# Infini-attention plus gated layer on one Trainium2 core: the second block's key features are turned by VectorE and moved within SBUF, and the key and query columns are put in another order

## The chip, the cores and the metric

The kernel runs on one core of a Trainium2 chip. The core has five engines that run their own instruction streams and wait for one another through semaphores: TensorE (PE in the profile; its weight loads are shown apart as PEld), VectorE (DVE), ScalarE (ACT), GpSimd (POOL) and SyncE (SP). SP issues most of the transfers here, POOL issues some; the transfers run on 16 DMA engines. SBUF is the working memory of 128 partitions, PSUM the memory of eight banks into which TensorE writes, DRAM the large memory outside.

The metric is the device time of one execution in microseconds (us), lower is better. Three executions of the kernel before took 670.75, 671.38 and 671.44 us; the median is 671.38 us.

## What is computed

```python
x = A_x                                   # 1 x 2048 x 448
xn = _layernorm(x, axis=-1)
return x + A_ref(xn, wq, wk, wv, wo, beta) + B_ref(xn, w_gate, w_up, w_down)

# A_ref: 16 heads of 28; the 2048 tokens are 4 blocks of 512
phi = lambda t: jnp.where(t > 0, t + 1.0, jnp.exp(t))
for s in range(4):
    qs, ks, vs = q[:, :, s], k[:, :, s], v[:, :, s]
    p = softmax(qs @ ks.T * scale + mask)             # inside the block
    a_dot = p @ vs
    a_mem = (phi(qs) @ M) / (phi(qs) @ z + 1e-6)      # what earlier blocks left
    outs.append(g * a_mem + (1 - g) * a_dot)
    M = M + einsum("bhld,bhle->bhde", phi(ks), vs)    # 28 x 28 for each head
    z = z + phi(ks).sum(tokens)
# B_ref: down(sigmoid(xn @ w_gate) * (xn @ w_up)), 1792 wide
```

The part that the change touches is the memory `M`, `z`: for each of the blocks 0, 1 and 2 the key features `phi(ks)` are multiplied with the values, summed over the block's 512 tokens. That sum runs over the partitions of a matmul, so the tokens have to lie on the partitions, whereas the keys come out of their projection with the columns (heads and their 28 rows) on the partitions and the tokens along the row. The key features have to be turned by 90 degrees first.

## The kernel before

**Stages.** A front stage goes through the four blocks `b` of 512 tokens. In each block it makes the values (`values`, four groups of 128 tokens, 11 matmuls each) and then the keys and queries (`keys_queries`, called for `c` = 0 to 6: seven chunks of 128 of the 896 key and query columns, keys first, 11 matmuls each with 512 moving columns). The precision is that of float32, made from a high and a low part of each operand, so each weight is split into a high part by ACT and a low part by POOL (`split_qk`). Behind the front stage lies a long stage in which the gated layer's matmuls, the attention inside the blocks and the output projection are interleaved by a table of ticks. The change edits nothing in the tick table.

**What sets the order.** PE, ACT and DVE execute the front stage in the order in which the code is written. SP and POOL are ordered by the framework's scheduler, and both issue transfers strictly one after another. Block 0 is written out by hand ahead of the loop up to its third group of values.

**The keys of a block.** For a key chunk `c` (0 to 3; the fourth has 64 key columns), `keys_queries` leaves the key features in a tile `e` (columns by tokens, 128 x 512): ACT copies the high part to `qk` (L413) and makes the exponential (L417, L418), DVE the low part (L419) and the feature (L424). At `k` = 3 and `k` = 5 `key_rows` has PE transpose two chunks each (L434, 16 transposes of 128x128 a block), and ACT copies them from PSUM to `kn` (L436). After the seventh chunk `update(b)` multiplies: 64 small matmuls (L445) with 28 columns of `kn` as weights and 32 columns of the values `vst` moving, and DVE adds the four strips to the memory `mst` (L452, L454).

**What else the prediction speaks of.** In block 0 the tokens of block 1 are normalised ahead: `statistics(1)` and `statistics(2)` (L324 to L326) are ready-made ahead of the first chunk, `normalise(1, k - 1)` (L350) makes the rows `xn`, of which POOL copies a tail (L356), and `turn(1, k - 3)` has PE transpose them (L103). For blocks 2 and 3 DVE turns the rows in 32x32 squares into a staging space (L359), and `spread` moves the squares with 16 transfers of 32 partitions each, 8 from SP and 8 from POOL (L374). From block 2 on `load_features` (L460, four transfers from SP) fetches the query features of the block before, which `keys_queries` wrote to DRAM (`fd`, L427), and `recall` (L467) multiplies them with the memory, right behind the block's first chunk.

## Time and profile before

| what | value |
|---|---|
| three executions | 670.75, 671.38, 671.44 us |
| the profiled execution, its own time | 671.5 us |
| its span, first to last instruction | 669.6 us |
| PE busy | 663.7 us (99% of the span) |
| DVE busy | 571.4 us (85%) |
| ACT, POOL busy | 336.1 us (50%), 147.4 us (22%) |
| transposes of the key features L434, x48 | 6.4 us of busy time |
| memory updates L445, x384 | 3.9 us |
| memory reads L467, x96 | 4.9 us |
| granted TensorE clock, whole span | 1.000 |

The share of busy time is no measure of a margin by itself: matmuls overlap, and a matmul that starts late because of a wait can still be drawn as one piece with those around it. In the prediction the rows of the timeline are read by their starts: the time from the start of one piece of PE work to the start of the next is what that piece cost. A row of the timeline gives the start in us from the span's start, the duration in us, the engine, the line of the kernel before, the operation, output and inputs, shapes, and how many instructions are merged into the row; an idle time ahead of it, with what ended it, stands in brackets.

### The profile page before, as it was taken

How to read it: one execution, taken by the hardware profiler on the slowest of the kernel's cores; microseconds unless marked ns; L12 is line 12 of the kernel's file. 1: busy time of each engine (PE TensorE's matmuls, PEld its weight loads, DVE VectorE, ACT ScalarE, POOL GpSimd, SP SyncE). 2: the span in 40 equal slices, each digit the busy share in tenths (PEclk: the TensorE clock that was granted, in tenths of full speed). 3: DMA queues.
4: the chain of work that ended last, by engine and by line, in shares of the span. 5: the costliest groups of instructions: out<-in, count | busy, mean ns of one | idle time of the engine just before them, and what ended most of it. 6: DMA issues, size and time to landing. Idle time of an engine off the chain costs nothing.

```text
span 669.6 us, 11201 instructions
## 1 busy us (share of the span) xinstructions
PE 663.7 (99%) x3922; PEld 553.2 (83%) x3922; DVE 571.4 (85%) x987; ACT 336.1 (50%) x560; POOL 147.4 (22%) x354
## 2 busy tenths in 40 slices
PE   8999999999999999999999999999999999999997
PEld 7888888778888888788787878788887887888897
DVE  6986695878999899899998999899998997999864
ACT  4848474423556455455645546455544644545220
POOL 3502210002222222233122322222122122321000
PEclk9999999999999999999999999999999999999999
DMA  8537788995523432324243423426243352323442
GB/s 321 221 128 251 238 287 284 309 273 197 144 73 88 109 93 73 103 57 105 74 96 103 89 72 57 128 52 141 57 103 64 92 115 57 86 78 80 112 153 97
DMA packets 48767, 88.09 MB, mean 132 GB/s; under 512 B 6856, under 2 KB 22856, under 8 KB 48200
## 3 DMA queue, kind: packets, MB, share of 16 engines
q1 hardware_dynamic: 45048, 79.01, 39.1%
q0 software_dynamic: 3520, 8.26, 6.1%
q8 instruction: 31, 0.51, 0.3%
q14 instruction: 24, 0.20, 0.1%
q10 hardware_dynamic: 144, 0.11, 0.0%
HBM read 52.89 MB, written 32.64 MB: 128 GB/s over the span
## 4 chain that ended last, share of the span: by engine, by line
PE 97%; DVE 2%; DMA 0%; ACT 0%; issue 0%; DVEq 0%
PE pgu L260 42%; PE pd L184 21%; PE pp L412 11%; PE st L704 6%; PE pa L790 5%; PE po L889 5%; PE pv L392 5%; PE pk L434 1%; PE pmm L445 1%; PE n L467 1%; DMA acc<-in_x 0%; DVE stats L324 0%; PE pt L103 0%; DVE xn L350 0%; DVE xs L110 0%
## 5 line engine op out<-in xcount | busy, mean ns | idle before, releaser
L260 PE MATMUL pgu<-xs,wgu 128*128 128x512 f32 x1232 | 301.2, 392 | 0.0
L260 PEld LDWEIGHTS pgu<-xs,wgu 128*128 128x128 f32 x1232 | 228.7, 188 | 46.6 <-issue 2.5
L184 PE MATMUL pd<-wdn,hh 128*128 128x448 f32 x672 | 155.3, 366 | 0.0
L184 PEld LDWEIGHTS pd<-wdn,hh 128*128 128x128 f32 x672 | 122.7, 188 | 11.6 <-issue 0.8
L719 POOL TENSOR_SCALAR_AFFINE_SELECT w<-w 128x256 f32<-128x256 f32 (+1 forms) x160 | 76.1, 479 | 224.0 <-ACT w L708 157.6
L772 ACT ACTIVATE w<-w 128x1024 f32<-128x1024 f32 (+1 forms) x96 | 87.8, 915 | 58.3 <-DVE w L768 58.1
L708 ACT ACTIVATE w<-st 128x512 f32<-128x512 f32 x128 | 75.6, 592 | 60.1 <-PE st L704 59.8
L768 DVE TENSOR_TENSOR w<-w,mb 128x1024 f32<-128x1024 f32 (+1 forms) x96 | 100.6, 1054 | 0.8
L726 DVE TRANSPOSE_TENSOR_REDUCE mx<-w 128x32 f32<-128x1024 f32 x64 | 78.9, 1233 | 4.9 <-POOL w L719 4.9
L412 PE MATMUL pp<-xs,wqk 128*128 128x512 f32 x308 | 73.7, 393 | 0.2 <-DVE kn L473 0.2
L186 DVE TENSOR_TENSOR acc<-pd,acc 128x448 f32<-128x448 f32 x112 | 67.4, 602 | 4.0 <-PE pd L184 4.0
L283 ACT ACTIVATE hh<-sg 128x512 fp32r<-128x512 f32 x56 | 35.3, 631 | 67.7 <-DVE sg L277 44.6
L412 PEld LDWEIGHTS pp<-xs,wqk 128*128 128x128 f32 x308 | 57.2, 188 | 12.9 <-issue 0.8
L704 PE MATMUL st<-qk 84*128 84x128 f32 (+3 forms) x256 | 62.0, 313 | 0.0
L267 ACT ACTIVATE sg<-pgu 128x512 f32<-128x512 f32 x56 | 33.2, 592 | 45.0 <-PE pgu L260 44.9
L704 PEld LDWEIGHTS st<-qk 84*128 84x128 f32 x256 | 47.9, 189 | 8.7 <-issue 1.4
L277 DVE SCALAR_TENSOR_TENSOR sg<-sg,pgu 128x512 f32<-128x512 f32 x56 | 37.7, 673 | 10.1 <-PE pgu L260 9.9
L754 DVE STREAM_TRANSPOSE mb<-top 128x1024 f32<-128x1024 f32 x32 | 39.5, 1234 | 3.3 <-POOL top L751 3.2
L286 DVE SCALAR_TENSOR_TENSOR hh<-sg,hh 128x512 fp32r<-128x512 f32 x56 | 38.2, 681 | 0.2 <-ACT hh L283 0.2
L419 DVE TENSOR_TENSOR qk<-pp,qk 128x512 fp32r<-128x512 f32 x28 | 19.2, 686 | 22.2 <-ACT e L417 21.6
L790 PE MATMUL pa<-w,vv 128*32 128x128 f32 (+3 forms) x512 | 37.8, 436 | 0.0
L392 PE MATMUL pv<-wv,xs 128*128 128x448 f32 x176 | 37.4, 367 | 0.3 <-POOL wv L508 0.2
(113 smaller groups left out, 607.2 us busy)
## 6 DMA issues: line engine op xcount, KB each, us to landing
qk<-qd SPq DMA_DIRECT2D x192, 112.0 KB
qd<-qk SPq DMA_DIRECT2D x28, 512.0 KB
raw<-in_w_ffn SPq DMA_DIRECT2D x14, 512.0 KB
acc<-in_x SPq DMA_DIRECT2D x5, 896.0 KB
vd<-vst SPq DMA_DIRECT2D x4, 1024.0 KB
vv<-vd SPq DMA_DIRECT2D x16, 256.0 KB
od<-w POOLq DMA_DIRECT2D x16, 256.0 KB, 4.1
sums<-od SPq DMA_DIRECT2D x32, 128.0 KB
```

Of the source, the lines that this page charges most:

```text
L184: T.matmul(pd[:, :D], l, r, start=n == 0, stop=n == len(mms) - 1)
L186: V.tensor_add(acc[b][:, t, :], pd[:, :D], acc[b][:, t, :])
L260: T.matmul(dst, wgu[f][:, w, side * P:(side + 1) * P], xs[b][:, a, :], start=n == 0, stop=n == len(TERMS) - 1)
L392: T.matmul(pv[:, :D], xs[b][:, a, t * P:(t + 1) * P], wv[w], start=n == 0, stop=n == len(TERMS) - 1)
L412: T.matmul(pp, wqk[c][:, w, :], xs[b][:, a, :], start=n == 0, stop=n == len(TERMS) - 1)
L704: T.matmul(st[:, at:at + L - kb * P], self.qk[:KS, 1, h, kb * P:(kb + 1) * P], self.qk[:KS, 0, h, kb * P:], start=True, stop=True)
L708: A.activation(w, st, AF.Copy)
L719: G.affine_select(d, d, pattern=pattern, base=0, channel_multiplier=-1, compare_op=ALU.is_ge, fill=MASK)
L726: V.tensor_reduce(self.mx[:, 32 * h:32 * h + 32], w3[:, h, :2 * L].rearrange("p (b n) -> p b n", n=32), axis=mybir.AxisListType.X, op=ALU. ...
L768: V.tensor_sub(w, w, m)
L772: A.activation(w, w, AF.Exp, scale=SCALE)
L790: T.matmul(pa[32 * j:32 * j + 32, kb * P:], self.vv[:, kb, 32 * j:32 * j + 32], self.pairs[j // 2].block(j % 2, kb), start=kb == 0, stop=k ...
```

## The change

**Columns.** The 448 key columns and the 448 query columns are now projected in the order row-major over heads (all 16 heads' row 0, then all heads' row 1, and so on) instead of head by head. The order is made when the weights are split: `split_qk` reads the raw weights with a step of 28 elements. One chunk of 128 columns now draws on the whole 448 raw columns of its side, so the raw weights lie in two tiles of 448 columns (keys, queries) and are loaded by eight transfers in pieces of 512 bytes (one of 64 columns a side), instead of seven chunks in pieces of 2 KB. The query side uses the space of `phi`. The chunks' splits come one chunk later (`split_qk(c + 3)` behind chunk `c`), and `statistics(2)` stands behind block 0's second chunk instead of ahead of its first. The readers of keys and queries in DRAM follow: a load of query features is now one run of 8 KB a partition (L503), and the last block's four loads are issued together.

**The memory update.** In all three blocks the values are now the weights (32 columns) and the key features move (28 columns, one head's rows, 16 elements apart). The result is the transposed memory, so DVE adds it in one instruction to a new tile `memory` and turns that in squares into `mst` (one more instruction), in place of four strips.

**Block 1.** `EXCHANGED = (1,)`: the 16 PE transposes of block 1 and the four ACT copies behind them are gone. DVE turns the four chunks `e` in 32x32 squares (L450) into the staging space that `spread(2)` has just emptied (the fourth into a tile of `e`), and 24 transfers within SBUF (12 from SP, 12 from POOL, 32 partitions each) bring the squares to their places in `kn`: 16 behind chunk 2, 8 behind chunk 3. `update(1)` is called behind the matmuls of the next block's first values instead of behind block 1's last chunk.

On PE, in blocks 1 and 2 (`pp` are the key and query chunks, `pk` the transposes, `pmm` the update, `pv` the values), before:

```order
L412 MATMUL pp<-xs_66,wqk_117 128x512 x11
L434 MATMUL pk<-ident,e 128x128 x8
L412 MATMUL pp<-xs_66,wqk_118 128x512 x11
...
L412 MATMUL pp<-xs_66,wqk_120 128x512 x11
L445 MATMUL pmm<-vst,kn 28x32 x64
L392 MATMUL pv<-wv,xs_67 128x448 x44
```

and now:

```order
L417 MATMUL pp<-xs_66,wqk_117 128x512 x11
L417 MATMUL pp<-xs_66,wqk_118 128x512 x11
...
L417 MATMUL pp<-xs_66,wqk_120 128x512 x11
L395 MATMUL pv<-wv,xs_67 128x448 x11
L490 MATMUL pmm<-kn,vst 32x28 x64
L395 MATMUL pv<-wv,xs_67 128x448 x33
```

The transposes are gone, and the update stands one group of values later.

On SP, from block 1's keys to block 2 (`qd` and `fd` are the stores of keys, queries and query features, `vd` that of the values, `stage<-acc_71` is `spread(3)`), before:

```order
L420 DMA qd_80<-qk 128x1024 x4
L427 DMA fd_84<-e 64x512
...
L460 DMA phi<-fd_84 28x4x512 x3
L398 DMA vd_89<-vst 128x2048
L374 DMA stage<-acc_71 32x4x128
```

and now:

```order
L425 DMA qd_80<-qk 128x1024 x3
L462 DMA kn<-phi 32x3x128 x8
L425 DMA qd_80<-qk 128x1024
L432 DMA fd_84<-e 64x512
L464 DMA kn<-e 32x128 x4
...
L377 DMA stage<-acc_71 32x4x128
L503 DMA phi<-fd_84 28x2048 x4
L401 DMA vd_89<-vst 128x2048
```

Twelve transfers of key features stand between the stores of chunks 2 and 4, and the four loads of query features now stand behind the first transfer of `spread(3)`.

On DVE, in block 0 (`acc_70` and `acc_71` are the tokens of blocks 1 and 2), before:

```order
L326 TENSOR_SCALAR vh_328<-mv_327 128x4
L324 BN_STATS stats_341<-acc_71 128x6
L325 BN_AGGR mv_342<-stats_341 128x2
...
L326 TENSOR_SCALAR vh_343<-mv_342 128x4
L419 TENSOR_TENSOR qk<-pp,qk 128x512
L424 SCALAR_TENSOR_TENSOR e<-pp,e 128x512
...
L625 TENSOR_SCALAR gate_n<-gate 128x4
...
L350 TENSOR_SCALAR xn<-acc_70,mv_327,y_338 128x16x7x4
```

and now:

```order
L329 TENSOR_SCALAR vh_328<-mv_327 128x4
L424 TENSOR_TENSOR qk<-pp,qk 128x512
L429 SCALAR_TENSOR_TENSOR e<-pp,e 128x512
...
L674 MEMSET memory 128x128
...
L678 TENSOR_SCALAR gate_n<-gate 128x4
...
L327 BN_STATS stats_397<-acc_71 128x6
L328 BN_AGGR mv_398<-stats_397 128x2
...
L329 TENSOR_SCALAR vh_399<-mv_398 128x4
L353 TENSOR_SCALAR xn<-acc_70,mv_327,y_338 128x16x7x4
```

The nine instructions of `statistics(2)` have moved from ahead of the first chunk's work to just ahead of the first rows `xn` of block 1.

The diff, cut to what this speaks of:

```diff
+EXCHANGED = (1,)
...
+        memory = sb.tile([P, HG, 32], F32, name="memory", bufs=1)
+        kn_blocks = kn.rearrange("p t n -> p (t n)")[:, :NT * D].rearrange("p (m t r) -> p m t r", t=NT, r=32)
...
         def values(b, t):
             pv = bank("pv", "p")
             value_terms(b, t, pv, EARLY[1] if b == 0 else TERMS)
+            if t == 0 and b - 1 in EXCHANGED:
+                update(b - 1)
             store_values(b, t, pv)
...
+        def turn_keys(e, et):
+            rows = et.shape[0]
+            V.transpose(et.rearrange("p (q t r) -> p t q r", q=4, t=NT),
+                        e[:rows].rearrange("p (t q n) -> p t q n", q=4, t=NT))
+
+        def send_keys(b, et=None):
+
+            to = kn_blocks.rearrange("p m t r -> p m (t r)")
+            src = stages[b + 1][:, :3 * L].rearrange("p (c q n) -> p c q n", c=3, q=4)
+            for q in range(4):
+                for i in range(4 if et is None else 2):
+                    queue = nc.sync if i % 2 else nc.gpsimd
+                    strip = slice(32 * i, 32 * i + 32)
+                    if et is None:
+                        queue.dma_start(to[32 * q:32 * q + 32, i:12:4, :], src[strip, :, q, :])
+                    else:
+                        queue.dma_start(to[32 * q:32 * q + 32, 12 + i, :], et[strip, P * q:P * (q + 1)])
...
         def update(b):
...
-                        T.matmul(pmm[32 * i:32 * i + DH, 32 * j:32 * j + 32], kn[:, t, DH * h:DH * (h + 1)],
-                                 vst[:, t, h, :], start=t == 0, stop=t == NT - 1)
...
+                        T.matmul(pmm[32 * i:32 * i + 32, 32 * j:32 * j + DH], vst[:, t, h, :], rows[t][h],
+                                 start=t == 0, stop=t == NT - 1)
+            p3, m3 = pmm[:, :P].rearrange("p (j c) -> p j c", c=32)[:, :, :DH], memory[:, :, :DH]
+            if b == 0:
+                V.tensor_copy(m3, p3)
+            else:
+                V.tensor_add(m3, p3, m3)
+            V.transpose(mst[(b + 1) % 2].rearrange("p j c -> p (j c)"), memory.rearrange("p j c -> p (j c)"))
...
+        raw_qk = [space.rearrange("p t n -> p (t n)")[:, :4 * D].rearrange("p (w n) -> p w n", w=4)
+                  for space in (stage, features())]
+        for side in range(2):
+            for c in range(4):
+                to, at = (P * c, 0) if side == 0 else (max(P * c - 64, 0), 64 if c == 0 else 0)
+                n = min(P, D - to) if side == 0 else P - at
+                nc.sync.dma_start(raw_qk[side][:, :, to:to + n],
+                                  w_qk[c + 3 * side].rearrange("p (w n) -> p w n", w=4)[:, :, at:at + n])
+            if side == 0:
+                nc.sync.dma_start(acc[1], x_block(1))
...
         def split_qk(c):
...
+                r = raw_qk[side].rearrange("p w (h r) -> p w r h", h=H)[:, :, r0:r1, :]
...
+                A.activation(hi, r, AF.Copy)
+                G.tensor_sub(lo, r, hi.bitcast(F32))
...
             for t in range(3 if b == 0 else 0, NT):
                 values(b, t)
                 if b == 0:
-                    split_qk(t)
                     mv, vh = statistics(1, 0, NT)
...
-                    st[2] = statistics(2, 0, NT)
...
-                if b == 0 and c + 4 < 7:
-                    split_qk(c + 4)
+                if b == 0 and c + 3 < 7:
+                    split_qk(c + 3)
+                if b == 0 and k == 1:
+                    st[2] = statistics(2, 0, NT)
...
-                    for i in range(NG):
-                        if k == (2, 3, 4, 4)[i]:
-                            load_features(b, i, phi)
+                    for i in range(NG if k == 4 else 0):
+                        load_features(b, i, phi)
...
-                if k in (3, 5):
+                if b in EXCHANGED:
+                    exchange(b, c)
+                elif k in (3, 5):
                     for c in (k - 3, k - 2):
                         key_rows(c, e[c])
-                if k == 6:
+                if k == 6 and b not in EXCHANGED:
                     update(b)
```

`exchange(b, c)` turns chunk 0 at `c` = 1, chunks 1 and 2 at `c` = 2 with the first 16 transfers, and chunk 3 at `c` = 3 with the other 8.

More of the change, by code (lines that the diff above doesn't have):

```diff
@@ L436, in key_rows, with turned, exchange @@
             A.activation(kn[:, :, c * P:c * P + n], pk.rearrange("p (t n) -> p t n", t=NT)[:, :, :n], AF.Copy)
+        def turned(b, c):
+            space = stages[b + 1].rearrange("p (c n) -> p c n", n=256)
+            return space[:, 2 * c:2 * c + 2, :].rearrange("p c n -> p (c n)")
+        def turn_keys(e, et):
[13 more added lines that the diff above has]
+                        queue.dma_start(to[32 * q:32 * q + 32, 12 + i, :], et[strip, P * q:P * (q + 1)])
+        def exchange(b, c):
+            if c == 1:
+                turn_keys(e[0], turned(b, 0))
+            elif c == 2:
+                turn_keys(e[1], turned(b, 1))
+                turn_keys(e[2], turned(b, 2))
+                send_keys(b)
+            elif c == 3:
+                et = sb.tile([P, L], F32, name="e", bufs=4)
+                turn_keys(e[3], et[:64])
+                send_keys(b, et)
         def update(b):
             pmm = bank("pmm", "m")
+            if b in EXCHANGED:
+                rows = [[kn_blocks.rearrange("p m t (c h) -> p m t c h", h=H)[:, :, t, :, h] for h in range(H)]
+                        for t in range(NT)]
+            else:
+                rows = [[kn[:, t, h:D:H] for h in range(H)] for t in range(NT)]
             for j in range(HG):
@@ L510, in split_qk @@
         def split_qk(c):
-            r = raw_qk[c].rearrange("p (c n) -> p c n", c=4)
-            A.activation(wqk[c][:, 0:4, :], r, AF.Copy)
-            G.tensor_sub(wqk[c][:, 4:8, :], r, wqk[c][:, 0:4, :].bitcast(F32))
+            for side in range(2):
+                j0, j1 = max(P * c, D * side), min(P * (c + 1), D * (side + 1))
+                if j0 >= j1:
+                    continue
+                r0, r1 = ((j - D * side) // H for j in (j0, j1))
+                r = raw_qk[side].rearrange("p w (h r) -> p w r h", h=H)[:, :, r0:r1, :]
+                hi, lo = (wqk[c][:, w:w + 4, j0 - P * c:j1 - P * c].rearrange("p w (r h) -> p w r h", h=H)
+                          for w in (0, 4))
+                A.activation(hi, r, AF.Copy)
+                G.tensor_sub(lo, r, hi.bitcast(F32))
         warm = bank("warm", "gu")
@@ L621 @@
                     if b == 0:
+                        V.memset(memory, 0.0)
                         A.activation(gate, gate, AF.Exp, scale=-1.0)
@@ L633 @@
                         phi = features()
-                    for i in range(NG):
-                        if k == (2, 3, 4, 4)[i]:
-                            load_features(b, i, phi)
+                    for i in range(NG if k == 4 else 0):
+                        load_features(b, i, phi)
                     if k > 4:
@@ L684, in load @@
                 for n in range(2):
[L685 to L687 removed]
+                    rows = qd[self.s][D * (1 - n):D * (2 - n), parts[n], :].rearrange("(r h) f -> r h f", h=H)
+                    nc.sync.dma_start(self.qk[DH * c:DH * (c + 1), n].bitcast(F32), rows[:, self.h0:self.h0 + 2, :])
         def block(self, h, kb):
```

24 lines of the change are left out of this document (4 added, 20 removed).

## The prediction

> **What bounds the kernel now.** I read the page first, then the chain of waits, then the timeline of each engine over the first 140 us.
>
> ```profile
> span 669.6 us, 11201 instructions
> PE 663.7 (99%) x3922; PEld 553.2 (83%) x3922; DVE 571.4 (85%) x987; ACT 336.1 (50%) x560; POOL 147.4 (22%) x354
> PE 97%; DVE 2%; DMA 0%; ACT 0%; issue 0%; DVEq 0%
> ```
>
> TensorE (PE) sets the end: 97% of the chain. Work taken off PE is won in full, and a wait put in front of PE in the front stage is lost in full, since no idle time lies behind it to take it up. The profiled execution took 671.5 us, the span and 1.9 us around it; the median of the runs is 671.4, so 0.1 is taken off at the end.
>
> The timeline of PE over blocks 0, 1 and the start of 2, where all edits lie:
>
> ```profile
> 19.68 10.14 PE L412 MATMUL pp<-xs,wqk 128*128 128x512 f32 x44
> 29.66 1.21 PE L434 MATMUL pk<-ident,e 128*128 128x128 f32 x8
> 30.71 0.64 PE L103 MATMUL pt<-ident,xn 128*128 128x128 f32 x4
> 31.10 2.77 PE L412 MATMUL pp<-xs,wqk 128*128 128x512 f32 x11
> ...
> 51.11 10.16 PE L412 MATMUL pp<-xs,wqk 128*128 128x512 f32 x44
> 61.11 1.03 PE L434 MATMUL pk<-ident,e 128*128 128x128 f32 x8
> 61.90 5.26 PE L412 MATMUL pp<-xs,wqk 128*128 128x512 f32 x22
> 67.01 1.03 PE L434 MATMUL pk<-ident,e 128*128 128x128 f32 x8
> 67.80 2.77 PE L412 MATMUL pp<-xs,wqk 128*128 128x512 f32 x11
> 70.49 1.29 PE L445 MATMUL pmm<-vst,kn 128*28 128x32 f32 x128
> 71.71 9.14 PE L392 MATMUL pv<-wv,xs 128*128 128x448 f32 x44
> 80.69 2.68 PE L412 MATMUL pp<-xs,wqk 128*128 128x512 f32 x11
> 83.30 1.22 PE L467 MATMUL n<-phi,mst 28*32 28x512 f32 x32
> ```
>
> From start to start: four chunks cost 10.00 us (51.11 to 61.11), so 2.50 each; the update 1.22 (70.49 to 71.71); a group of values 8.98 / 4 = 2.245; block 2's first chunk with its wait 2.61.
>
> **Term 1, the transposes that go: -1.88 us.** Block 1's keys take 19.38 us now (51.11 to 70.49). Without the transposes they are seven chunks, 7 x 2.50 = 17.50. The four PSUM banks of the chunks allow this: DVE's last use of a chunk ends some 2.7 us behind its last matmul (the row of 60.60 below, against 58.61 = 51.11 + 3 x 2.50), far less than the 7.5 us until chunk 6 starts in the same bank. The four ACT copies that go were off the path.
>
> **Term 2, the statistics of block 2, moved: +2.96 us.** This looks like bookkeeping, and I think it is the largest term. The rows that carry it, from the timelines of DVE, ACT and POOL in block 0:
>
> ```profile
> 21.26 0.17 DVE L326 TENSOR_SCALAR vh<-mv 128x4 f32<-128x4 f32 x1
> 21.34 0.62 DVE L324 BATCH_NORM_STATS2 stats<-acc 128x6 f32<-128x448 f32 x1
> 24.59 0.69 DVE L419 TENSOR_TENSOR qk<-pp,qk 128x512 fp32r<-128x512 f32 x1
> 26.00 0.72 DVE L343 TENSOR_TENSOR tm<-y 128x4 f32<-128x4 f32 x1
> 28.01 0.96 DVE L625 TENSOR_SCALAR gate_n<-gate 128x4 f32<-128x4 f32 x1
> 30.08 0.50 DVE L350 TENSOR_SCALAR xn<-acc,mv,y 128x448 f32<-128x448 f32 x1
> ...
> 21.67 1.28 ACT L586 ACT_TABLE_LOAD   x1
> 23.55 0.59 ACT L417 ACTIVATE e<-pp 128x512 f32<-128x512 f32 x1
> ...
> 25.41 1.30 POOL L513 TENSOR_TENSOR wqk<-wqk_raw,wqk 128x512 fp32r<-128x512 f32 x1 [2.79 <-ACT wqk L512]
> 27.66 1.29 POOL L513 TENSOR_TENSOR wqk<-wqk_raw,wqk 128x512 fp32r<-128x512 f32 x1 [0.95 <-ACT wqk L512]
> 30.72 0.24 POOL L356 COPY xn<-xn 128x64 f32<-128x64 f32 x1 [1.78 <-DVE xn L350]
> ```
>
> Now DVE is never idle here: block 2's statistics (21.34 to 24.59, 3.25 us) fill the time in which ACT loads a table and evacuates the first chunk. DVE's low part (L419) needs ACT up to the end of L417 at 24.14. With the statistics gone from there it starts at about 24.15 instead of 24.59, 0.44 earlier, and DVE idles for 2.7 us (21.43 to 24.15) that nothing else fills. The 3.25 us come back directly ahead of block 1's first rows `xn` (L350, ends 30.58), with a memset of some 0.15 (as the small row of 21.26): 30.58 - 0.44 + 3.25 + 0.15 = 33.54. POOL's copy of the tail follows in the same step as now (30.72 + 0.24), and PE, whose transposes (L103) read `xn` at 30.71 and go on at 31.10, is at that place in time either way. So PE's next chunk starts 2.96 us later. What queues behind the waiting transposes is all of PE.
>
> Bounds: two small DVE operations (26.00, 28.01) now last until POOL's subtraction ends (26.71, 28.95), 1.3 us too much for their size, and DVE idles 0.5 ahead of the gate; if all this vanished in the new order, 1.2 would stay. If POOL holds DVE three times for 0.4 more, 4.2.
>
> **Term 3, the update of block 1 waits for its transfers: +1.7 us.** The rows:
>
> ```profile
> 60.60 0.69 DVE L424 SCALAR_TENSOR_TENSOR e<-pp,e 128x512 f32<-128x512 f32 x1
> 63.81 0.51 SPq L427 DMA_DIRECT2D fd<-e  x1
> ...
>   ACT e L417: 21.6, 13
> ...
> L478 DVE STREAM_TRANSPOSE tb<-kn x4: 702/707/711, 125.7 to 151.1; 128x512 f32<-128x512 f32 x4
> L374 SPq DMA_DIRECT2D stage<-phi x8: 597/604/1312, 49.1 to 53.8; - x8
> L374 POOL DMA_DIRECT2D stage<-phi x8: 557/558/746, 49.3 to 53.4; - x8
> L420 SPq DMA_DIRECT2D qd<-qk x28: 319/320/531, 25.3 to 136.9; - x28
> DMA to landing us min/median/max: 2.1/2.6/3.2
> ```
>
> (The last is for tile phi: POOL's quiet transfers of squares. SP's show no landing; I take the same.) In the times of the old span, before any shift: chunk 2's feature ends at 61.29; two turns of 0.7 end at 62.6. SP then issues eight transfers of the same kind as those of L374, 0.60 and a gap of 0.05 each, 5.3 with the first: 67.9. Then, in the order of its queue, chunk 3's store and feature store (0.32 + 0.51 and gaps), 68.9; then four small ones of 32 runs each, by the nearest rows 0.32 to 0.60: the last starts between 70.1 and 70.9 and lands 2.1 later, 72.2 to 73.0. POOL, 12 at 0.56 from 62.9, lands at about 71.8. PE arrives at 51.11 + 17.50 + 2.245 = 70.86. The wait is 1.3 to 2.2; I take 1.7. Were the last transfers to take the longest landing of the `spread(3)` transfers (4.9, next fence) it would be 4.5; with a quicker SP landing, 0.6. DVE's turns cost nothing on PE: ahead of the chunks' low parts DVE waits for ACT (13 times, 21.6 us in all, the idle row of L419), 1.7 a time, so at most two turns too many for one chunk are made up in the next.
>
> **Term 4, block 2's memory read waits for its features: +0.45 us.**
>
> ```profile
> 78.62 0.99 DVE L359 STREAM_TRANSPOSE acc<-xn 128x448 f32<-128x448 f32 x1
> L460 SPq DMA_DIRECT2D phi<-fd x12: 307/329/1712, 70.4 to 132.3; - x12
> DMA to landing us min/median/max: 1.9/3.0/4.9
> ```
>
> Now these four loads are issued by 77.8, long ahead of the read at 83.30. In the new order they queue on SP behind the first transfer of `spread(3)`, which waits for DVE's last turn of block 3's rows (ends 79.61, that is 7.9 us after the update ended at 71.71). DVE's work behind the update gets 0.6 shorter and there is no key work ahead of it that outlasts the update, so call the update's end U: turn done at U + 6.0, the transfer U + 6.65, four loads from U + 7.0 to U + 8.1, landed 2.6 later, U + 10.7. PE reaches the read at U + 3 x 2.245 + 2.61 = U + 9.35, its fourth part 0.9 later: U + 10.25. The wait is 0.45; nothing if landing takes 2.1, 2.7 if it takes 4.9.
>
> **Term 5, three updates with strided features: +0.45 us.** 28 columns in place of 32 move: 1.22 / 8 = 0.15 less each at best. Against it the moving elements now lie 64 bytes apart, and no row shows PE reading so. The nearest is DVE's turn that writes in steps of 16 bytes, 0.98 for 448 elements (78.62 above), against 0.71 for 512 without steps (L478), 1.59 times as long an element. Put on the whole update: 1.22 x 0.875 x 1.59 = 1.70, 0.48 more. Half way, 0.15 each. At worst twice the streaming, 0.9 each. [...]
>
> **Costed at nothing.** The weights in pieces of 512 bytes: the key half is needed at ACT's first split.
>
> ```profile
> 15.72 0.61 ACT L512 ACTIVATE wqk<-stage 128x512 fp32r<-128x512 f32 x1
> 10.00:20.00 10.00, 9.67 (x50) 8.15 (x50) 8.22 (x24) 5.44 (x14) 5.22 (x5) 1.00 0.99 380
> ```
>
> Half of 1.8 MB at the 380 GB/s of that stretch is 2.4 us from some 7 us on; even twice that ends at 12, with 3.7 to spare. The cover is thinnest for the gate's tiny loads, last in line: PE loses up to 1 us if they come 3 us later. The strided splits: POOL's subtraction of chunk 3 must be done by 27.4 (chunk 3's second matmul, 19.68 + 3 x 2.50 + 2.50 / 11) and starts about where the row of 25.41 stands, so it may last 2.0 against 1.30. The last block's loads: the same bytes, issued a little later, in longer runs; that read waits even now, so up to 1 us either way.
>
> The sum: -1.88 + 2.96 + 1.7 + 0.45 + 0.45 = +3.68. 671.5 + 3.7 - 0.1 = **675.1 us**.
>
> **Rivals.**
>
> (a) DVE's late rows cost nothing, because its 2.7 us idle are refilled (ACT finishing the first chunk about 2.5 us sooner, or the held operations vanishing with it). For: DVE had slack of such a kind twice. Against: ACT's table load ends at 22.95 whatever DVE does. Then +0.7: 672.1 us, no change. It decides if `xn` is done by 31.
>
> (b) Both waits for transfers vanish too and only PE's own work counts: -1.88 + 0.45 = -1.4, 670.0 us, faster. For it: SP's queue would have to be through by 68.8, and `xn` in time. Against it: SP's count of transfers alone.
>
> (c) POOL's strided subtraction becomes the bound in block 0. At 2.6 us, twice now, chunk 3's low part is 0.6 late, which hides in term 2's wait, and DVE is held 1.3 longer twice: 3.68 + 2.6 = +6.3, 677.7 us. It decides from 2.0 us on. For it: the reads go from whole runs to steps of 112 bytes. [...]
>
> (d) The updates stream at half the rate and the landings are long: +0.9 x 3 in place of 0.45 and 2 more in term 3: +7.9, 679.3 us.
>
> That the change doesn't do what it says is excluded by the order of the instructions: the 16 transposes are gone.
>
> **How the numbers follow.** Forecast 55%, its own range 672.5 to 677.5 (term 2 from 1.2, term 3 to 3). (a) 20%, (b) 8%, (c) 11%, (d) 6%. The range 671.3 to 678.8 takes in the forecast, most of (a) and (c) and leaves out (b) and (d). About 0.2%, 1.3 us, is what a measurement can tell from no change. Faster: (b) and a little of (a), 0.10. Same: most of (a) and the forecast's low edge, 0.20. Slower: the rest, 0.70.
>
> **What would show it.** On PE's timeline of the changed kernel: the start of block 0's fifth chunk near 34 (now 31.10), ahead of it a wait on DVE's `xn` or POOL's copy; block 1's seven chunks in 17.5 us; a gap of 1 to 2 us between the first and second group of block 2's values, ended by a transfer into `kn`; the update's length from start to start, 1.1 to 1.7; the read (L467 now, L511 then) longer than 1.22. If the fifth chunk starts by 31.5, term 2 is wrong and (a) holds; if no gap stands at the update, term 3 is.

## The result and the profile after

The changed kernel takes **688.68 us** (median of six runs, 685.52 to 690.82) against 670.96 of the kernel before (six runs, 670.62 to 671.44): 1.0262 times as long, 95% interval 1.0234 to 1.0290. That is +17.7 us where +3.7 was forecast. The profiled execution is the quickest of the six, 685.52 us. TensorE (PE) still sets the end. The page of the changed kernel, its span and the shares of its chain of waits:

```profile
span 683.7 us, 11222 instructions
...
PE 90%; DMA 3%; DVE 3%; ACT 2%; SPq 1%; issue 1%; DVEq 0%; ACTq 0%
```

PE has gone from 97% to 90% of the chain: waits now stand between its matmuls. The timeline of PE in the changed kernel, to set beside that of before (start, length, instructions, idle time ahead and what ended it):

```profile
28.23 2.56 PE L417 MATMUL pp<-xs,wqk 128*128 128x512 f32 x10 [0.66 <-POOL wqk L565]
30.64 1.03 PE L439 MATMUL pk<-ident,e 128*128 128x128 f32 x8
34.61 0.71 PE L104 MATMUL pt<-ident,xn 128*128 128x128 f32 x4 [2.94 <-DVE xn L353]
35.08 2.79 PE L417 MATMUL pp<-xs,wqk 128*128 128x512 f32 x11
...
44.58 1.82 PE L490 MATMUL pmm<-kn,vst 128*32 128x28 f32 x128
46.33 0.66 PE L104 MATMUL pt<-ident,xn 128*128 128x128 f32 x4
...
55.63 17.64 PE L417 MATMUL pp<-xs,wqk 128*128 128x512 f32 x77
73.11 2.37 PE L395 MATMUL pv<-wv,xs 128*128 128x448 f32 x11
77.67 1.93 PE L490 MATMUL pmm<-kn,vst 128*32 128x28 f32 x128 [2.18 <-DMA kn<-e]
79.53 7.51 PE L395 MATMUL pv<-wv,xs 128*128 128x448 f32 x33
86.87 2.68 PE L417 MATMUL pp<-xs,wqk 128*128 128x512 f32 x11
90.37 1.06 PE L511 MATMUL n<-phi,mst 28*32 28x512 f32 x8 [0.82 <-DMA phi<-fd]
91.61 1.06 PE L511 MATMUL n<-phi,mst 28*32 28x512 f32 x8 [0.18 <-DMA phi<-fd]
92.88 2.33 PE L511 MATMUL n<-phi,mst 28*32 28x512 f32 x16 [0.21 <-DMA phi<-fd]
95.14 9.10 PE L417 MATMUL pp<-xs,wqk 128*128 128x512 f32 x33
104.08 1.03 PE L439 MATMUL pk<-ident,e 128*128 128x128 f32 x8
...
150.43 1.22 PE L511 MATMUL n<-phi,mst 28*32 28x512 f32 x16
152.30 1.95 PE L511 MATMUL n<-phi,mst 28*32 28x512 f32 x16 [0.65 <-DMA phi<-fd]
154.18 10.97 PE L261 MATMUL pgu<-xs,wgu 128*128 128x512 f32 x47
```

Start to start, against the same stretches of the kernel before, the 14.1 us between the two spans (683.7 and 669.6) stand in these places:

| stretch of PE | before | after | us |
|---|---|---|---|
| start to block 0's fifth chunk | 31.10 | 35.08 | +3.98 |
| updates of blocks 0 and 2 | 1.22, 1.21 | 1.75, 1.75 | +1.07 |
| block 1's seven chunks, with or without transposes | 19.38 | 17.48 | -1.90 |
| wait ahead of the update of block 1 | 0 | 2.31 | +2.31 |
| that update and the three groups of values behind it | 7.96 | 9.20 | +1.24 |
| block 2's first chunk | 2.61 | 3.50 | +0.89 |
| block 2's memory read | 1.15 | 4.77 | +3.62 |
| the three chunks behind it | 7.62 | 8.94 | +1.32 |
| block 3's last memory read | 2.30 | 3.75 | +1.45 |

The first group of values of block 2 costs the same in both; the last 0.1 is in small rows. Two rows of the table (the update with the three groups, and the three chunks) got slower with no wait among their matmuls. Stretches of the changed kernel, with the clock that PE was granted as the fourth number behind the times (length, busy and count come first; the DMA share and GB/s follow):

```profile
74.00:77.40 3.40, 1.49 (x8) 1.00 0.54 177
77.60:80.80 3.20, 3.13 (x131) 0.50 1.01 383
81.00:94.40 13.40, 12.19 (x74) 1.00 0.72 221
94.60:97.80 3.20, 3.20 (x10) 0.50 0.73 234
98.00:150.00 52.00, 51.80 (x387) 1.00 0.79 270
```

PE ran at half its clock twice, for 3.41 us each, just behind the two places where it had waited for transfers. No term of the prediction held this.

The mean clock is also what tells the six runs apart: 0.995 in the quickest, 0.987 in the two slowest. The span times its mean clock is an estimate of the span that the same work and waits would have needed at full clock (the clock is given to 0.001, which is 0.7 us here). It is 679.8 to 681.3 in all six; in the 28 executions of the kernel before that stand beside the experiments it is 668.1 to 669.9, 669.0 in the mean. So of the 17.7 us some **11.5 are there at full clock and 6.2 are half clock**. The split is good to about 1 us: in the profiled execution the clock makes the two stretches cost 3.4 us, but the rows give 2.3 (0.7 in the update and the values behind it, 0.3 in the read, 1.3 in the three chunks), since the update, 1.86 us from start to start there, was hardly slower than the 1.75 of the others. The table of all runs:

| kernel | median, us | ratio to before (95%) | mean clock | span by clock (mean) |
|---|---|---|---|---|
| before | 671.0-671.3 | | 0.999-1.000 | 669.0 |
| the change | 688.68 | 1.0262 (1.0234-1.0290) | 0.987-0.995 | 680.5 |
| e1 statistics back | 686.62 | 1.0232 (1.0217-1.0247) | 0.987-0.989 | 677.2 |
| e2 no exchange | 680.22 | 1.0139 (1.0114-1.0164) | 0.992-1.000 | 676.4 |
| e3 loads first | 685.98 | 1.0217 (1.0185-1.0248) | 0.989-0.995 | 679.0 |
| e4 before, statistics late | 674.43 | 1.0046 (1.0031-1.0061) | 0.997-0.999 | 670.7 |
| e5 fills, misplaced | 689.20 | 1.0280 (1.0255-1.0304) | 0.989-0.995 | 682.7 |
| e6 reads reversed | 686.72 | 1.0234 (1.0219-1.0250) | 0.989-0.998 | 680.4 |
| e7 contiguous updates, memory wrong | 690.46, one run | | 0.987 | 679.7 |
| e8 splits early too | 686.99 | 1.0239 (1.0223-1.0255) | 0.987-0.993 | 678.5 |
| e9 more fills, misplaced | 688.79 | 1.0271 (1.0254-1.0288) | 0.994-1.000 | 685.1 |
| e10 stores on POOL | 683.85 | 1.0185 (1.0169-1.0200) | 0.991-0.997 | 676.8 |
| e11 plain splits, order wrong | 685.28, one run | | 0.989 | 676.0 |
| e12 combined | 682.80 | 1.0172 (1.0150-1.0194) | 0.989-0.996 | 675.8 |
| e13 fills in place | 684.25 | 1.0195 (1.0180-1.0211) | 0.999-1.000 | 682.1 |
| e14 small pieces | 693.55 | 1.0338 (1.0321-1.0355) | 0.983-0.987 | 680.9 |
| e16 combined again | 679.79 | 1.0138 (1.0115-1.0161) | 0.992-0.997 | 674.7 |

Because the clock differs from run to run, the readings below go by single rows of a profile or by the last column; medians alone mislead (e2 is 8.5 us below the change by its median and 4.1 by the last column).

### The profile page after: what moved, and what is told of

The parts are those of the page before. It is cut to its first block, busy times and chain, and to the rows that moved or that the text cites. A ratio compares the mean times of both kernels' runs of the same rounds, so it can differ in the third digit from the quotient of the medians.

```text
span 683.7 us, 11222 instructions
## 1 busy us (share of the span) xinstructions
PE 669.8 (98%) x3906; PEld 555.3 (81%) x3906; DVE 574.2 (84%) x986; ACT 338.1 (49%) x557; POOL 156.4 (23%) x367
## 4 chain that ended last, share of the span: by engine, by line
PE 90%; DMA 3%; DVE 3%; ACT 2%; SPq 1%; issue 1%; DVEq 0%; ACTq 0%
PE pgu L261 41%; PE pd L185 20%; PE pp L417 8%; PE st L757 6%; PE pa L843 5%; PE po L942 5%; PE pv L395 3%; DMA phi<-fd 2%; DMA acc<-in_x 1%; PE pmm L490 1%; ACT wqk L564 1%; PE n L511 1%; DVE acc L362 1%; DVE stats L327 0%; ACT qk L418 0%
```

## The experiments

**Block 0: is it the place of the statistics, or the splits?** Four runs. First, the statistics put back (e1), and the kernel before with only the statistics moved (e4):

```diff
@@ e1, from the changed kernel: beside block 1's statistics
+                    st[2] = statistics(2, 0, NT)
@@ behind the chunk
-                if b == 0 and k == 1:
-                    st[2] = statistics(2, 0, NT)
```

> The changed kernel with one thing undone: block 2's statistics stand ahead of block 0's first chunk again, as in the kernel before. Theory: term 2 is the place of the statistics and nothing else. The fifth chunk of block 0 then starts at 31.1 us in place of 35.1 and the time falls by 4.0 us, from 688.7 to about 684.7. Rival: the strided splits hold VectorE and ScalarE wherever the statistics stand (the changed kernel's fifth chunk came 1.0 us later than term 2's sum said). Then the chunk starts at about 32.1 and the time falls by 3.0 us only, to 685.7. Second rival: the statistics are not the cause, the splits alone are: under 1 us.

> The kernel before with one edit: block 2's statistics moved to where the change has them, behind the second chunk of block 0. Theory: the place of the statistics by itself costs what term 2 said, 2.96 us (fifth chunk at 34.06 in place of 31.10), 673.9 us. Rival 1: all 4.0 us that the changed kernel loses there come from it: 675.0. Rival 2: VectorE makes it up and the strided splits are what delayed the changed kernel: under 1 us, below 672.

In e1 the fifth chunk starts at 32.48, later than both the theory (31.1) and its rival (32.1) had it: 2.6 us of the 3.98 go, 1.4 stay. In e4, PE's timeline:

```profile
32.70 0.71 PE L103 MATMUL pt<-ident,xn 128*128 128x128 f32 x4 [1.87 <-DVE xn L350]
33.16 2.79 PE L412 MATMUL pp<-xs,wqk 128*128 128x512 f32 x11
```

33.16 in place of 31.10: the place alone costs 2.06, not the 2.96 expected. Its median is 3.2 up, with a clock of 0.997 in three of its four runs. So something else costs 1.4 with the statistics early (e1) and 1.9 with them late (3.98 - 2.06). Next, e1 with the splits one chunk earlier, as before (e8), and this with splits that read whole runs (e11, whose weights have their columns in the wrong order):

```diff
@@ e8, from e1: ahead of the first chunk, and in the loop
+                    split_qk(3)
-                if b == 0 and c + 3 < 7:
-                    split_qk(c + 3)
+                if b == 0 and c + 4 < 7:
+                    split_qk(c + 4)
@@ e11, from e8
-                r = raw_qk[side].rearrange("p w (h r) -> p w r h", h=H)[:, :, r0:r1, :]
+                r = raw_qk[side][:, :, j0 - D * side:j1 - D * side]
```

> The changed kernel with block 2's statistics ahead of the first chunk again and, in addition, the splits of the weights one chunk earlier, as the kernel before had them (chunk 3's ahead of the first chunk). With the statistics alone put back the fifth chunk started at 32.48 us in place of 31.10, and PE waited 0.65 us for chunk 3's low part. Theory: what is left of it is the longer splits holding VectorE: the 0.65 goes, but VectorE's xn still lasts until POOL's subtraction ends; the fifth chunk starts at 31.8 to 32.2 and the time falls by 0.3 to 0.7 us against that run, 686.1. Rival: the lateness of the splits was all: 31.1 to 31.4, 685.4.

> The run with block 2's statistics and the splits both early, and now the splits read whole runs of 128 (or 64) columns in place of every sixteenth's order; the weights' columns stand in the wrong order for that reason. Theory: what is left of block 0's loss (fifth chunk at 32.5 us in place of 31.1) is the strided reads alone: ScalarE's 1.2 us and POOL's 1.58 for 128x512 go back to 0.62 and 1.30, VectorE's xn is held no longer, and the chunk starts at 31.1 to 31.4. Rival: the two halves of the split (two instructions for the middle chunk) or the memset hold the order: it stays at 32.5.

PE's and VectorE's (DVE's) rows of e8, with one of POOL's subtractions, and then those of e11:

```profile
32.05 0.71 PE L104 MATMUL pt<-ident,xn 128*128 128x128 f32 x4 [0.33 <-DVE xn L353]
32.52 2.77 PE L417 MATMUL pp<-xs,wqk 128*128 128x512 f32 x11
...
21.56 1.19 DVE L329 TENSOR_SCALAR vh<-mv 128x4 f32<-128x4 f32 x1
...
27.51 1.47 DVE L347 TENSOR_TENSOR tm<-tm,vh 128x4 f32<-128x4 f32 x1
...
30.93 1.07 DVE L353 TENSOR_SCALAR xn<-acc,mv,y 128x448 f32<-128x448 f32 x1
...
30.21 1.54 POOL L565 TENSOR_TENSOR wqk<-phi,wqk 128x512 fp32r<-128x512 f32 x1 [1.24 <-ACT wqk L564]
```

```profile
30.53 0.60 PE L104 MATMUL pt<-ident,xn 128*128 128x128 f32 x4
30.88 2.77 PE L417 MATMUL pp<-xs,wqk 128*128 128x512 f32 x11
...
28.87 0.51 DVE L353 TENSOR_SCALAR xn<-acc,mv,y 128x448 f32<-128x448 f32 x1
```

Earlier splits change nothing (32.52, where 31.8 to 32.2 was expected); plain reads give all of it back (30.88, and xn 0.51 in place of 1.07). It is the strided reads: ScalarE (ACT) takes 1.25 for what took 0.61, POOL 1.54 to 1.61 for 1.30. What reaches PE is that DVE is held. Three of its operations in e8 last until a subtraction of POOL ends, or a little longer: vh (1.19, in e11 0.17), the second tm (1.47; in e11 it was the first, with 0.72, so the pair takes 0.75 more) and xn (1.07, in e11 0.51), which began in the middle of POOL's 1.54 (30.21 to 31.75) and ended at 32.00. With vh starting 0.30 later than in e11 they make up all of xn's delay of 2.62 (29.38 in e11): 0.30 + 1.02 + 0.75 + 0.56 = 2.63. DVE was not idle in between, so no wait for ACT is part of it. In the changed kernel vh was held in the same way, from 21.23 to 22.41; ACT's table load stands behind an operation that reads vh and began at 22.66, where it was 21.67 before the change. The prediction had "costed at nothing" for these splits.

**Is the exchange behind the later waits?** The exchange undone, all else as changed:

```diff
-EXCHANGED = (1,)
+EXCHANGED = ()
```

> The changed kernel with block 1's keys transposed by TensorE again (16 transposes, ScalarE's copies), everything else as changed: late statistics, strided features in the updates, weights by columns, the new feature loads. Theory: the waits of update(1) (2.3 us) and of block 2's memory read (3.6 us, and 0.9 in the chunk ahead of it), and the half-clock stretches behind them (0.6 and 1.3 us) all come from the exchange; against them stand 1.9 us of transposes that come back. From the kernel before: 671.0 + 4.0 (statistics) + 1.7 (three updates) + 1.5 (block 3's memory read) = 678.2 us. Rival: block 2's read is late because its loads and spread(3) share queues whatever the keys do: then 3.6 to 5.8 us more, 682 to 684.

The median of 680.2 lies between the theory's 678.2 and the rival's 682; the quickest run, at a clock of 1.000, took 678.7. The rows decide for the theory: there is no wait at the update of block 1, and block 2's read takes 1.15 from start to start, with no wait ahead of it:

```profile
88.55 1.22 PE L511 MATMUL n<-phi,mst 28*32 28x512 f32 x32
```

At full clock it is 676.4, which is 4.1 under the change although 1.9 of transposes came back. Block 3's last read stays long (3.94 us from start to start), so that is not the exchange.

**What makes block 2's loads late?** In the changed kernel SP issues:

```profile
67.09 5.08 SPq L462 DMA_DIRECT2D kn<-phi  x8
...
73.50 2.63 SPq L464 DMA_DIRECT2D kn<-e  x4
...
80.46 0.72 SPq L432 DMA_DIRECT2D fd<-e  x1
85.58 0.65 SPq L377 DMA_DIRECT2D stage<-acc  x1
86.67 1.62 SPq L503 DMA_DIRECT2D phi<-fd  x4
```

The loads are issued 7.1 us behind the update's end (79.53), as the prediction said. Two things stand ahead of them: the first transfer of `spread(3)` (85.58), and the last feature store (80.46). e3 moves the first away; e10 both:

```diff
@@ e3 and e10: spread
-                    queue = nc.sync if i % 2 else nc.gpsimd
+                    queue = nc.sync if i % 2 and b == 2 else nc.gpsimd
@@ e10: the feature stores
-                    nc.sync.dma_start(fd[b][lo:(c + 1) * P - D], e[D + lo - c * P:])
+                    (nc.gpsimd if b == 1 else nc.sync).dma_start(fd[b][lo:(c + 1) * P - D], e[D + lo - c * P:])
```

> The changed kernel with all 16 transfers of spread(3) issued by POOL, so that no transfer that waits for VectorE stands ahead of block 2's four feature loads on SP. Theory: the loads are issued by 81 us in place of 86.7 and landed by 86, ahead of the read at 90; the 3.6 us of waiting there, the half-clock stretch behind it (1.3 us) and some 0.9 us ahead of it go: 688.7 - 5.8 = 682.9. Rival 1: the loads land late because they share the DMA engines with the values' store and spread(3): the wait stays over 1.5 us and the time over 685. Rival 2: the half clock does not come from the wait but comes every so many us: then only 3.6 go, 685.1.

> The changed kernel with block 1's four feature stores issued by POOL and all 16 transfers of spread(3) too. With spread(3) alone moved, SP still waited until 87.0 us for the last feature store, which it had issued at 82.4 behind twelve sends and three stores of 512 KB. Theory: the sends on SP, which push the feature stores back by some 5 us, are what makes block 2's loads late; with the stores on POOL the last one is issued by 78, the loads by 83, and the read of block 2 takes 1.2 us in place of 4.8, the chunk ahead of it 2.6 in place of 3.5: 4.5 us less at full clock and 1 to 2 less of half clock, 688.7 - 6 = 682.7. Rival: the DMA engines are full there (share 1.0 from 78 to 82 us) and the store lands as late from POOL: the read still takes over 3 us, 686.

e3: a miss. The loads go out at 87.20, with the update's end at 81.33, only 1.3 us sooner than in the change. SP itself waits until then for the feature store that it had issued at 82.38. The read still takes 3.44 and the span by clock falls by 1.5. e10, PE's timeline:

```profile
79.28 1.79 PE L490 MATMUL pmm<-kn,vst 128*32 128x28 f32 x128 [3.53 <-DMA kn<-e]
81.00 8.70 PE L395 MATMUL pv<-wv,xs 128*128 128x448 f32 x33
...
92.12 1.22 PE L511 MATMUL n<-phi,mst 28*32 28x512 f32 x32
93.27 7.78 PE L417 MATMUL pp<-xs,wqk 128*128 128x512 f32 x33
```

The loads go out 2.2 us behind the update's end (83.19, 81.00) and the read is back at 1.15. So what stood ahead of them on SP is the cause; as e3 shows, the transfer of `spread(3)` alone is not, and the stores behind the sends have to go too, as the theory said. But the sends now land later: the update waits 3.53 in place of 2.18, with half clock behind it. Of the 6 us expected 4.8 came, 3.7 of them at full clock.

**Why does a read with 1.2 us of waits take 4.8?** The rows of the change say it already: eight matmuls, one group of rows, take 1.06 us alone; all 32 take 1.15 when they stand back to back. Loads that land one by one make four groups of it. e6 takes the groups in reverse:

```diff
-            for i in range(NG):
+            for i in reversed(range(NG)):
                 for j in range(HG):
                     T.matmul(n2[i]
```

> The changed kernel with the memory read's four groups of rows taken in the order 3, 2, 1, 0, while the loads still come in the order 0, 1, 2, 3. Theory: the four groups use different rows of the array and run side by side when they stand back to back (1.15 us for all), but each alone takes 1.06; loads that come one after the other made block 2's read 4.77 us long though its rows show only 1.2 us of waiting. Reversed, PE waits once, for the last load, and then reads all four in 1.15 us: block 2's read ends 0 to 1.1 us earlier, block 3's 0.3 to 1.0 earlier, 687.3 in the middle. Rival: the groups do not overlap and the read is slow because of the clock: no change in its end, 688.7, or worse, since PE is idle in one piece and the clock drops more often: up to 690.

```profile
94.92 2.12 PE L511 MATMUL n<-phi,mst 28*32 28x512 f32 x32 [4.89 <-DMA phi<-fd]
```

One wait of 4.89 and one read (of 2.12, since its end lies at half clock); it ends no sooner, where the theory had 0 to 1.1 us, but 1.4 us later counted from the update's end (80.01 to 96.97, in the change 79.53 to 95.14): the last load lands about when the last group had started. Block 3's last read waits 1.92 and then takes 1.27, 0.6 less in all, as expected. The groups do run side by side, but for block 2 that only moves the wait. The span by clock is that of the change.

**Is it idle time that halves the clock?** Matmuls of no use put where PE waits. In e5 and e9 the fills meant for block 2's read stood at block 3's first read, which waits for nothing; e13 has them in place.

```diff
@@ e13, in the places named (e5: 12, 9, 3, reads in order; e9: 12, 15, 20 at block 3's first read, 6 ahead of the two others)
+            if t == 0:
+                fill(12, pt)                 # block 1's first transposes
+            if b in EXCHANGED:
+                fill(15, pmm)                # update of block 1
+            fill({1: 17, 2: 0, 3: 10}[b], n2[3])   # reads of block 2 and, last, block 3
-            for i in range(NG):
+            for i in reversed(range(NG)):
```

> The changed kernel with matmuls of no use (identity by identity, 0.21 us each, into a bank that the next matmul overwrites) put where PE now waits: 12 ahead of block 1's first transposes in block 0, 9 ahead of the update of block 1, 3 ahead of block 2's memory read. No wait gets shorter for it: what PE waited for still comes when it comes. Theory: the half clock of 3.4 us comes from PE having stood idle for much of a stretch just before. Then the mean clock goes from 0.987-0.995 to 0.998 or more and the time from 688.7 to 682.5 (span by clock stays at 680.5, and 1.9 around it). Rival 1: the half clock comes from the updates and reads themselves (narrow matmuls that use a part of the array) or from the transfers: then the clock stays as it is and the time at 688 or, with fills that last longer than the waits, above. Rival 2: the read's serial pieces still trigger it: one stretch stays, 684.

> As the run with fills, but the fills now cover the waits in full: 12 in block 0, 15 ahead of the update of block 1, 20 ahead of block 2's memory read and 6 ahead of block 3's, with the groups of both reads in the order 3, 2, 1, 0, so that PE waits once. In the first run with fills the half clock behind the update was gone (33 value matmuls in 6.71 us in place of 7.34), while the read, hardly covered, still had one of two stretches behind it. Theory (idle time of PE triggers the half clock): the mean clock is 0.998 or more in every run and the span 681 to 683, the time 683 to 685. Rival (the clock drops for what runs there, not for idle time): the clock stays near 0.991, the time at 688 to 690.

> The changed kernel with fills where PE waits: 12 in block 0, 15 ahead of the update of block 1, 17 ahead of block 2's memory read (the two runs before had these at block 3's first read, which waits for nothing) and 10 ahead of block 3's last read; the groups of the reads in the order 3, 2, 1, 0. Theory (idle time of PE triggers the half clock): the mean clock is 0.997 or more in every run, the span 681 to 683 (680.5 at full clock and up to 1.5 of fills that last longer than the waits), the time 683 to 685. Rival: the clock stays at 0.987 to 0.995 and the time at 688.

e5: the values behind the update are quick again (80.53 to 87.24, 6.71), block 2's read has two stretches behind it; 689.2, nothing won. e9: clock 0.994 to 1.000, but 4.6 us of fills at the wrong read (128.28 to 132.84), so 688.8 in place of the 683 to 685 expected. e13, its read of block 2:

```profile
94.42 1.25 PE L517 MATMUL n<-phi,mst 28*32 28x512 f32 x32 [0.55 <-DMA phi<-fd]
95.59 7.78 PE L420 MATMUL pp<-xs,wqk 128*128 128x512 f32 x33
```

The clock is 0.999 or 1.000 in all four runs and the time 684.25, in the range that idle time as the trigger gave (683 to 685). The waits are all still there: the read ends at 95.59, in the change at 95.14. The reversed reads alone (e6) had left the span by clock as it was. PE gained 4.4 us by doing more work.

**What does an update cost?** e7 reads each head's features from neighbouring columns, which belong to several heads, so that its memory is a wrong one:

```diff
-                rows = [[kn[:, t, h:D:H] for h in range(H)] for t in range(NT)]
+                rows = [[kn[:, t, DH * h:DH * (h + 1)] for h in range(H)] for t in range(NT)]
```

> The changed kernel, but each update reads the features of a head from 28 neighbouring columns (which belong to several heads) in place of every sixteenth column; the memory is a wrong one for that reason, all else is computed as before. Theory: term 5's step of 64 bytes in the moving operand is what makes an update 1.75 us: it falls to 1.07 (28 of 32 columns of the 1.22 of the kernel before), some 2.0 us in all. Rival: the exchange of the operands (values as weights, features moving) costs it: the update stays at 1.75. Between the two: part each.

```profile
46.33 1.29 PE L490 MATMUL pmm<-kn,vst 128*32 128x28 f32 x128
47.55 0.66 PE L104 MATMUL pt<-ident,xn 128*128 128x128 f32 x4
```

1.22, as before the change: neither 1.07 nor 1.75. The step of 64 bytes costs 0.53 an update; the exchange of the operands and 28 columns in place of 32 together change nothing.

**The shape of the loads.** e14 cuts each load into 112 pieces:

```diff
-            nc.sync.dma_start(phi[32 * i:32 * i + DH], rows)
+            nc.sync.dma_start(phi[32 * i:32 * i + DH][:, ::-1, :], rows[:, ::-1, :])
```

> The changed kernel with one thing changed: each of the twelve feature loads takes its four heads in the reverse order on both sides, so that the same 224 KB move as 112 pieces of 2 KB, as in the kernel before, and not as 28 pieces of 8 KB. Theory: the shape makes the loads land late (the packets of 8 KB took 0.42 to 0.46 us each, those of 2 KB 0.10): block 3's last read falls from 3.75 to about 2.3 us, block 2's from 4.8 by 1 to 2, in all 2.5 to 3.5 us less: 685 to 686. Rival: it is the issue alone, which comes after the last feature store has landed: nothing changes, 688.7.

The theory fell, and the rival's "nothing changes" too: it is 4.9 us worse, nearly all of it half clock (680.9 at full clock, against 680.5). SP now takes 0.80 us an issue where it took 0.38 (tile phi in e14, then in the change):

```profile
L504 SPq DMA_DIRECT2D phi<-fd x12: 792/804/935, 87.7 to 150.3; - x12
```

```profile
L503 SPq DMA_DIRECT2D phi<-fd x12: 324/384/847, 86.7 to 145.8; - x12
```

Block 3's last read took longer still (154.24 to 158.99), with half clock behind it. So smaller pieces do not make the reads earlier; that they also take twice as long to issue leaves the shape by itself untested. For block 3's last read the cause is argued, not shown: its four loads are issued in one row from 143.96, at most 6.5 us ahead of the read, where the kernel before had issued the first two 12.5 and 9.4 us ahead (125.43 and 128.44, read at 137.88), and the DMA engines are at 0.92 of their time or more from 144 to 154 us.

**What is left when the named stalls are mended.** e12: statistics and splits early, stores and `spread(3)` on POOL, the update of block 1 behind the second group of values. e16: the same without the late update, with the pieces of e14.

```diff
@@ e12, in values()
+            if late and t == 0:
+                held.append(pv)
+                return
+            if late and t == 1:
+                update(b - 1)
+                store_values(b, 0, held.pop())
```

> The changed kernel with each stall mended that the runs so far have named: block 2's statistics and the splits early, block 1's feature stores and spread(3) on POOL, and the update of block 1 behind the second group of values in place of the first (2.25 us later, against a wait of 2.2 to 2.3). Theory: what is left against the kernel before is the sum of four terms at full clock: transposes -1.9, strided splits +1.4, three updates +1.6, block 3's read +1.5, in all +2.6: 673.8 us, with a clock of 0.998 or more. Rival: the waits come back elsewhere (the third group of values waits for ScalarE's copy behind the update, the read of block 2 follows the update and is as late): 678 or more.

> Statistics and splits early, block 1's feature stores and spread(3) on POOL, loads in pieces of 2 KB, the update of block 1 in its place behind the first group of values. Theory: against the kernel before at full clock transposes -1.9, strided splits +1.4, updates +1.6, wait of the update +3.5 (the sends land later with the stores among them), block 3's read 0 to +0.3: +4.7, 676 us, and 1 to 2 us of half clock behind the update: 677 to 678. Rival: block 3's read keeps its 1.3 us (the pieces are not the cause): 679.

e12 missed by 9: the update still waits 1.28, and behind it PE stands still with nothing that the profile can name:

```profile
82.71 5.55 PE L395 MATMUL pv<-wv,xs 128*128 128x448 f32 x19 [3.78 <-issue]
```

e16 took 679.8, the rival's 679: block 3's last read kept its length (143.87 to 147.84). It is the best version of the change and 1.0138 times the kernel before, so none beats it.

## Why the prediction was wrong

The direction was right, the size was not. Four steps failed: the clock had no term (5 to 6 us of the median), term 4 was put at 0.45 and came to 4.2 at full clock, the strided splits were "costed at nothing" and cost 1.4 to 1.9, and the last block's loads cost 1.45 where "up to 1" was allowed. By its steps:

- **Term 1** (-1.88): measured -1.90. Right.
- **Term 2** (+2.96, 1.2 to 4.2): alone it is +2.06 (e4). As its lower bound allowed, a hold vanished in the new order: the last gate row took 0.17 us in place of 0.96, and DVE's idle 0.48 ahead of the gate went with it, while the other held row grew from 0.72 to 1.07 (3.25 - 0.30 - 0.79 - 0.48 + 0.35 = 2.03).
- **The strided splits** ("costed at nothing"): with them 3.98 were lost in block 0. They cost 1.4 by themselves (e1, e8, e11) and 1.9 behind the late statistics. Only the deadline of POOL's subtraction was looked at, not that it holds DVE for longer. The deadline was missed too: chunk 3's low part was due at 27.4 and done at 28.18, and PE waited 0.66 for it; without that wait (e8) the fifth chunk starts no sooner, so it hid in the wait for xn. This is how rival (c) had it, but with the wrong condition: POOL took 1.5 to 1.6, under the 2.0 from which it was to decide. The steps made the subtraction of 128x512 about a fifth longer, 1.30 us (e11) to 1.54-1.61 (e8).
- **Term 3** (+1.7, 0.6 to 4.5): 2.31. The count of SP's queue was right.
- **Term 4** (+0.45, 0 to 2.7): the chunk and the read took 4.5 more, about 0.3 of it half clock, so 4.2 in place of 0.45. This is the wait that was mis-sized most. Its issue time came true, U + 7.1, though for two causes, of which only one was named. Its landing of 2.6 did not: the first load was there 3.7 behind its issue and the third 5.4 (87.48 to 92.88), with the DMA engines at 0.92 of their time from 86.6 to 92.9. And the sum took the wait for the last part alone, where groups that come one by one take 1.06 each.
- **Term 5** (+0.45): +1.6, by e7 all of it the step (1.75 against 1.22 an update). The half-way value between two bounds was wrong; the upper one (0.48) was close to the 0.53 of e7.
- **"The last block's loads, up to 1 us either way"**: +1.45. Four loads in a row behind the last store are the likely cause; e2 excludes the exchange, and pieces of 2 KB did not shorten it (e14, e16).
- **No term** held the clock: 6.2 us of the median by the mean clock, about 1 less by the rows. Without it the sum of what was measured, -1.9 + 4.0 + 1.6 + 2.3 + 4.2 + 1.45, is +11.7, against 11.5 by the spans at full clock and 11.8 by the rows of the profiled execution (14.1 - 2.3).

Rival (a) is excluded by the start of 35.08; its own counter-argument, that ACT's table load ends at 22.95 whatever DVE does, did not hold either, since the table load came behind the held vh and ended at 23.94. Rival (b) is excluded by the two waits for transfers; (d) had the long landings, but not at the place where they cost most, and its +0.9 an update, at half the rate, was an assumption that no run shows (+0.53).

## What to carry to other kernels

A wait put in front of a saturated TensorE is to be priced with the clock that may follow it: here 2.0 us of standing still were followed by 3.41 at half clock, which by that length cost up to 1.7 more (an estimate; the rows show 0.7), and runs of one kernel differ in it (mean clock 0.987 to 0.995 in the change, 0.992 to 1.000 in e2), so look at the mean clock of each run before comparing medians. Transfers that are added to a queue are to be priced by what stands behind them: here the sends cost 2.3 us themselves and 4 more through the stores and loads that queued behind. A new access pattern is a cost for each engine that reads it (here ACT 0.61 to 1.25 us, POOL 1.30 to 1.54-1.61, PE 1.22 to 1.75 an update), and for an engine that is held meanwhile, as VectorE was here until POOL had ended (xn 1.07 us in e8, 0.51 in e11).

## What the hardware showed that was not expected

**The half clock comes on a fixed grid.** In the change it ran from 77.49 to 80.90 and from 94.55 to 97.96 us (read in steps of 0.05): 3.41 each, and 17.06 = 5 x 3.41 apart. In e1, e6, e7, e8 and e14 the starts are whole steps apart too: 17.1 and 58.0 us in e1 (5 and 17 x 3.41), 17.1 in e6 (5), 61.4 in e8 (18). What seems to count is how little PE did in one such window of 3.41 us. The stall of block 0, 2.94 us, fell across two windows in the change (1.45 and 1.49) and nothing followed; in e3 a stall of the same length lay with 2.5 us in one window:

```profile
32.60:35.80 3.20, 0.90 (x6) 1.00 0.00 0
36.00:39.20 3.20, 3.20 (x9) 0.50 0.54 216
39.40:80.20 40.80, 38.62 (x358) 1.00 0.55 183
80.40:83.60 3.20, 3.20 (x82) 0.50 1.03 387
```

35.83 and 80.20 are 13 x 3.41 apart. Ahead of the change's first stretch 2.0 us of idle time in 3.41 were enough (75.48 to 77.49). In e10, whose wait of 3.53 us fell across two windows, 1.92 were not enough; 1.61 in the next window, with the update's narrow matmuls behind them, were.

**A busy row need not count as busy.** Ahead of the second stretch PE was busy by its rows for nearly all of the window:

```profile
91.20:94.40 3.20, 2.81 (x28) 1.00 0.93 307
```

but with the read's narrow matmuls (28 rows by 32 columns), one group of rows at a time. Side by side, in 1.2 us and with no wait ahead, the same matmuls had no stretch behind them: the clock stayed at 1.00 behind block 3's first read (1.26 us in e8 and e14, 1.27 in e10) and behind block 2's (1.22 in e10). e8 has the same picture ahead of a stretch of 6.8 us, and in e1, e3, e8 and e14 block 3's last read has one in it or behind it after 0.25 to 0.58 us of idle time in the window; in the change, with 0.65, it has none. That the narrow shape is the reason is inferred from such places and was not tried by itself.

**Open:** the 3.78 us of e12 without a releaser. The spans by clock of its four runs (675.0 to 676.2) lie some 3 us above the sum of its other terms (669.0 - 1.9 + 1.4 + 1.6 + 1.3 + 1.3 = 672.7), so it seems to be there in each; no run tells its cause.
